# Three chunks loaded in float32 by another queue, one burst of column tiles, and an instruction order from a list scheduler that runs when the program is built, in a fused retention and feed-forward kernel

## The chip, the cores and the metric

The kernel runs on one core of one Trainium2 chip. Times are device microseconds (us) of one execution; with one core, the slowest core is that core. Before the change the median of four timed runs was 247.65 us (247.22 to 248.03). The span of a profile, from the first to the last instruction, is 1 to 3 us shorter than the time of its run.

The engines are called PE (TensorE, matmuls), ACT (ScalarE), DVE (VectorE), POOL (GpSimd) and SP (SyncE, here only an issuer of DMAs). "Granted clock" is the share of full TensorE clock that the profile records. Time without a record counts as full, so read it with care: in the traces the first record lies at 27 to 45 us, and until about then matmuls run at about half pace (four 128-column ones last 0.61 us and later 0.39).

## The reference, cut to what matters

```python
def _attn_ref(q, k, v):                       # 4 x 8 heads x 768 x 64, f32
    gamma = 1.0 - 2.0 ** (-5.0 - np.arange(H))
    for t in range(S):                        # retention, one step at a time
        state = gamma * state + k_t (outer) v_t
        y[:, :, t] = scale * q_t @ state

def _moe_ref(x, w_in, w_out, alpha):          # 3072 tokens, 512 -> 2048 -> 512
    h = x @ w_in
    s = np.sin(alpha * h)
    g = h + s * s / (alpha + 1e-09)
    return g @ w_out
```

(Shortened here.) Both kernels cut the sequence into 24 chunks of 128 tokens. Inside a chunk the recurrence becomes matmuls: q and k are scaled by powers of gamma, both are transposed ("T"), the scores k·q are masked ("A"), the mix is scores·v plus q·state ("Y"), and the state takes k·v on ("S"). The chunks then go through the feed-forward in groups of up to four (512 tokens): per group 16 *input slots* of four matmuls each (into `ph`), a sine and a square on ACT, a sum on DVE (into `gT`), and per chunk 16 *output* matmuls (into `po`).

## The kernel before

The parts that the change and the argument touch; cuts are marked with `# ...`.

```python
groups = [2, 4, 4, 4, 4, 4, 2]
# ...
def load_chunk(j):                            # q, k, v of one chunk: POOL issues, cast to bf16 on the way
    # ...
    for name, src in (("q", q), ("k", k), ("v", v)):
        t = big.tile([128, H, D], BF16, name=f"{name}r", tag=f"{name}r", bufs=NJ)
        nc.gpsimd.dma_start(out=t, in_=src[b, :, c * C:(c + 1) * C, :].rearrange("h s d -> s h d"))
# ...
def stage_Y(j):                               # mix: state part on the full array, then score part in column tiles
    # ...
    if c > 0:
        for p in range(NP):
            nc.tensor.matmul(py[:, p, :], s_bd[c % 2][:, p, :], st["qkT", j][:, p, :], ...)
    for p in range(NP):
        for e in range(2):
            nc.tensor.matmul(py[64 * e:64 * e + 64, p, :], raw["v", j][:, 2 * p + e, :], st["aT", j][:, e, p, :], ...)
    # ...
# ...
loads = [w_in 0..3], chunks 2 3, [w_out 0 1], chunks 4 5, [w_out 2 3], chunks 6.. # (shortened)
# ...
for g in range(NG + 1):                       # the instruction order: input slots and output matmuls alternate,
    # ...
    for i in range(FF):                       # and the stages T, A, Y, S of the next group are spread between them
        if g < NG:
            ph = ff_in(g, i)
            s = ff_act(g, i, ph)
        lo, hi = na * i // FF, na * (i + 1) // FF
        for j, sidx in att[lo:hi]:
            if sidx == 0:
                if loads:
                    loads.pop(0)()
                if j + 1 < NJ:
                    stage_scale(j + 1, nc.vector if j + 1 < 6 else nc.gpsimd)
            stages[sidx](j)
        if g < NG:
            ff_add(g, i, ph, s)
        if g > 0:
            # ...
            ff_out(g - 1, i * n, n)
```

Two things to keep in mind: the order in which each engine gets its instructions is fixed when the program is built, and each engine runs its own in order. An instruction that has to wait holds up everything behind it on that engine.

## Time and profile before

| | before |
|---|---|
| median time | 247.65 us (four runs) |
| span of the profile, mean granted clock | 246.4 us, 0.986 |
| PE busy | 217.6 us (88%) |
| first matmul / first input slot | 11.01 / 21.69 us |
| ninth chunk's transposes on PE | 66.05 us |
| last 36 output matmuls | 234.38 to about 242.3 us |

The page of the profile cuts the span into 40 slices. A digit is the busy share of a slice in tenths; PEclk is the granted clock in tenths of full speed.

```profile
PE   0146748799999999999999999999999999999993
PEclk9999986999999999999999999999999999999999
DMA  9999999999998879849957965901101110012112
```

PE is at 9 tenths from about the ninth slice on (a slice is 6.2 us). Before that it waits, and in that time the DMA engines are full. The sixth and seventh slice show a stretch at a lower clock (34.75 to 41.6 us in the clock records).

The chain of work that ended last, followed back from the end, gives shares of the span:

```profile
PE 72%; DMA 12%; ACT 5%; POOL 5%; issue 2%; DVE 2%; POOLq 0%
```

So PE is the limit for most of the span, and DMA with POOL for the start. What one chunk costs PE is read from the timeline of PE. Columns: start, duration, engine, line, operation, output and inputs, count, and in brackets the idle time before it with what ended it.

```profile
106.36 0.39 PE L134 MATMUL pt<-ident,qs 128*128 128x128 bf16 x4
...
106.81 1.03 PE L218 MATMUL po<-w_out,gT 128*128 128x512 bf16 x4
107.67 1.03 PE L195 MATMUL ph<-xT,w_in 128*128 128x512 bf16 x4
108.63 0.40 PE L145 MATMUL pa<-qkT 64*128 64x128 bf16 x8
...
113.10 0.39 PE L176 MATMUL ps<-vr,ks 128*128 128x128 bf16 x4
...
115.05 0.39 PE L134 MATMUL pt<-ident,qs 128*128 128x128 bf16 x4
```

From one transposition to the next is 115.05 - 106.36 = 8.69 us. Four long matmuls take 0.86 us from start to start (107.67 - 106.81), and the eight such blocks of a chunk 6.9 us; about 1.77 us is left for T, A, Y and S. The scores at 108.63 start 0.96 us after the block ahead of them and not 0.86: 0.10 us is lost where PE goes from the full array to 64-row tiles.

The timeline of POOL shows the loads of the start. A DMA that has to wait names the DMA that it waited for:

```profile
8.83 3.04 POOL L74 DMA_DIRECT2D w_in<-in_moe_w_in_dram  x4
11.83 0.92 POOL L66 DMA_DIRECT2D qr<-in_q_dram  x1
...
17.02 0.88 POOL L66 DMA_DIRECT2D vr<-in_v_dram  x1 [0.78 <-DMA w_in<-in_moe_w_in_dram]
19.53 0.75 POOL L77 DMA_DIRECT2D w_out<-in_moe_w_out_dram  x1 [1.62 <-DMA w_in<-in_moe_w_in_dram]
```

Counted through, the DMA at 17.02 us is POOL's sixteenth and waits for its eighth; the next waits for its ninth. So in these traces POOL has no more than eight of its DMAs under way: an issue can be held until the eighth one before it has landed, and POOL, being in order, does nothing else while it is held.

### The profile page before, as it was taken

What the parts mean: (1) busy time and instruction counts of PE and PEld (TensorE: products, weight loads), DVE (VectorE), ACT (ScalarE), POOL (GpSimd) and SP (SyncE); (2) the same over time, 40 slices, a digit from 0 to 9 for tenths busy, and PEclk for the clock granted to TensorE, in tenths of its full rate; (3) what the DMA queues carried; (4) which work ended last, traced back from release to release, by engine and by line L of the source; (5) the groups of instructions that cost most, each with busy time, mean ns of one, the idle gap of its engine ahead of it and who ended that gap; (6) DMA issues with size and microseconds to landing.
All of it is one profiled execution on the core that took longest, in us unless ns stands there. A gap on an engine that the chain in (4) does not pass through costs nothing.

```text
span 246.4 us, 4059 instructions
## 1 busy us (share of the span) xinstructions
PE 217.6 (88%) x1568; PEld 115.8 (47%) x1568; DVE 132.8 (54%) x208; ACT 172.1 (70%) x294; POOL 108.5 (44%) x127
## 2 busy tenths in 40 slices
PE   0146748799999999999999999999999999999993
PEld 0134436544554555445555544555454454466541
DVE  0444646675666654674475466447645556353431
ACT  2325458889888887778778776877877786877710
POOL 8974754899977733763574376303000000000000
PEclk9999986999999999999999999999999999999999
DMA  9999999999998879849957965901101110012112
GB/s 53 117 205 177 193 164 194 118 95 78 88 133 55 92 85 67 87 66 72 99 67 85 64 80 73 80 26 45 43 0 47 43 43 22 23 43 85 45 43 85
DMA packets 84642, 20.18 MB, mean 82 GB/s; under 512 B 77456, under 2 KB 81552, under 8 KB 84624
## 3 DMA queue, kind: packets, MB, share of 16 engines
q0 software_dynamic: 79104, 13.64, 70.6%
q1 hardware_dynamic: 5520, 6.30, 7.3%
q8 instruction: 12, 0.20, 0.3%
q14 instruction: 6, 0.05, 0.1%
HBM read 27.27 MB, written 6.29 MB: 136 GB/s over the span
## 4 chain that ended last, share of the span: by engine, by line
PE 72%; DMA 12%; ACT 5%; POOL 5%; issue 2%; DVE 2%; POOLq 0%
PE po L218 33%; PE ph L195 29%; DMA w_out<-in_moe_w_out_dram 5%; DMA w_in<-in_moe_w_in_dram 4%; DMA vr<-in_v_dram 3%; PE pt L134 3%; PE py L163 3%; ACT s L202 3%; PE pa L145 2%; ACT s L203 2%; PE py L159 1%; POOL qr L66 1%; PE ps L176 1%; POOL kr L66 1%; DVE gT L207 1%
## 5 line engine op out<-in xcount | busy, mean ns | idle before, releaser
L207 DVE TENSOR_TENSOR gT<-ph,s 128x512 bf16<-128x512 f32 (+1 forms) x112 | 68.7, 613 | 83.5 <-ACT s L203 83.5
L195 PE MATMUL ph<-xT,w_in 128*128 128x512 bf16 (+1 forms) x448 | 104.6, 358 | 2.1 <-DVE gT L207 1.8
L202 ACT ACTIVATE s<-ph,alpha_sb 128x512 f32<-128x512 f32 (+1 forms) x112 | 70.0, 625 | 42.9 <-PE ph L195 30.8
L218 PE MATMUL po<-w_out,gT 128*128 128x512 bf16 x384 | 98.9, 380 | 0.0
L203 ACT ACTIVATE s<-s,rsq_alpha 128x512 f32<-128x512 f32 (+1 forms) x112 | 74.0, 661 | 3.6
L195 PEld LDWEIGHTS <-w_in 128*128 128x128 bf16 x448 | 44.3, 101 | 47.4 <-issue 4.4
L218 PEld LDWEIGHTS <-gT 128*128 128x128 bf16 x384 | 33.2, 98 | 29.1
L126 POOL TENSOR_TENSOR qs<-qr,qg 128x512 bf16<-128x512 bf16 x18 | 18.9, 1050 | 50.5 <-issue 46.1
L148 DVE TENSOR_TENSOR aT<-pa,mask 128x1024 bf16<-128x1024 f32 x24 | 29.3, 1221 | 4.6 <-PE pa L145 4.6
L66 POOL DMA_DIRECT2D qr<-in_q_dram x24 | 22.5, 938 | 1.3 <-POOLq L280 0.8
L66 POOL DMA_DIRECT2D vr<-in_v_dram x24 | 21.7, 905 | 0.8 <-DMA w_in<-in_moe_w_in_dram 0.8
L66 POOL DMA_DIRECT2D kr<-in_k_dram x24 | 21.6, 899 | 0.0
L134 PE MATMUL pt<-ident,qs 128*128 128x128 bf16 x96 | 10.2, 234 | 11.8 <-DVE qs L126 11.7
L166 ACT CAST xT<-py 128x512 bf16<-128x512 f32 x24 | 13.7, 570 | 9.8 <-PE py L163 9.8
L222 DVE COPY o_sb<-po 128x512 f32<-128x512 f32 x24 | 16.4, 681 | 5.0 <-PE po L218 5.0
L127 POOL TENSOR_TENSOR ks<-kr,kg 128x512 bf16<-128x512 bf16 x18 | 18.8, 1043 | 0.0
L136 DVE COPY qkT<-pt 128x1024 bf16<-128x1024 bf16 x24 | 16.4, 682 | 2.5 <-PE pt L134 2.4
L145 PE MATMUL pa<-qkT 64*128 64x128 bf16 x192 | 10.4, 233 | 7.5 <-DVE qkT L136 7.5
L134 PEld LDWEIGHTS <-qs 128*128 128x128 bf16 x96 | 7.8, 105 | 16.9 <-DVE qs L126 12.2
L182 ACT CAST s_bd<-ps 64x256 bf16<-64x256 f32 x40 | 14.3, 359 | 0.3
L145 PEld LDWEIGHTS <-qkT 64*128 64x128 bf16 x192 | 5.9, 100 | 17.0 <-DVE qkT L136 11.9
L163 PE MATMUL py<-aT,vr 128*64 128x128 bf16 x192 | 10.8, 239 | 3.0 <-DVE aT L148 2.4
(32 smaller groups left out, 77.1 us busy)
## 6 DMA issues: line engine op xcount, KB each, us to landing
out_dram<-o_sb SPq DMA_DIRECT2D x24, 256.0 KB, 2.0
qr<-in_q_dram POOLq DMA_DIRECT2D x24, 128.0 KB, 3.6
kr<-in_k_dram POOLq DMA_DIRECT2D x24, 128.0 KB, 4.4
vr<-in_v_dram POOLq DMA_DIRECT2D x24, 128.0 KB, 4.4
w_in<-in_moe_w_in_dram POOLq DMA_DIRECT2D x4, 512.0 KB, 8.0
w_out<-in_moe_w_out_dram POOLq DMA_DIRECT2D x4, 512.0 KB, 10.4
alpha_sb<-in_moe_alpha_dram SPq DMA_DIRECT2D x1, 8.0 KB, 3.0
```

The source lines that it names most:

```text
L66: nc.gpsimd.dma_start(out=t, in_=src[b, :, c * C:(c + 1) * C, :].rearrange("h s d -> s h d"))
L126: eng.tensor_mul(qs, raw["q", j], qg[:, c, :, None].to_broadcast([128, H, D]))
L127: eng.tensor_mul(ks, raw["k", j], kg[:, c, :, None].to_broadcast([128, H, D]))
L134: nc.tensor.transpose(pt[:, i * NP + p, :], t[:, 2 * p:2 * p + 2, :].rearrange("p h d -> p (h d)"), ident)
L145: nc.tensor.matmul(pa[:, e, p, :], qkT[r, NP + p, :], qkT[r, p, :], start=(p == 0), stop=True, skip_group_check=True)
L148: nc.vector.tensor_mul(aT.rearrange("p e n t -> p (e n) t"), pa.rearrange("p e n t -> p (e n) t"), mask_bc)
L163: nc.tensor.matmul(py[64 * e:64 * e + 64, p, :], raw["v", j][:, 2 * p + e, :], st["aT", j][:, e, p, :], start=(c == 0 and p == 0), stop=Tr ...
L195: nc.tensor.matmul(ph, w_in[:, i, f * 128:(f + 1) * 128], xT[g][:, i, :], start=(i == 0), stop=(i == KS - 1))
L202: nc.scalar.activation(out=s, in_=ph, func=ACTF.Sin, scale=alpha_sb[:, f:f + 1])
L203: nc.scalar.activation(out=s, in_=s, func=ACTF.Square, scale=rsq_alpha[:, f:f + 1])
L207: nc.vector.tensor_add(gT[g][:, f, :], ph, s)
L218: nc.tensor.matmul(po[g], gT[g][:, f, ts * C:(ts + 1) * C], w_out[:, f, :], start=(f == 0), stop=(f == FF - 1))
```

## The change

The intent, by its parts: (1) the first three chunks come in float32 through SP's queue, so that POOL need not issue them (POOL then scales their k and casts their v, DVE scales their q, and ACT copies their transposes, which DVE did before); (2) groups 3,4,4,4,4,4,1 instead of 2,4,4,4,4,4,2; (3) scores, mix and state of a chunk follow one another on PE, with mix and state in column tiles; (4) the order of all instructions comes from a list scheduler in the kernel's own code, which keeps a clock per engine from a simple cost model as it emits; (5) the square of a slot goes to DVE where the scheduler's clock has ACT far behind, and the last copy is split between DVE and ACT. With this, `ph` and `po` share four PSUM buffers, where each had two of its own.

The diff, cut to its core (cuts marked with `...`, some lines joined; most of the stage functions, the PSUM pools and the constants are left out):

```diff
+class Clock:
+    ...
+    def run(self, eng, us, *deps):
+        start = max([self.t[eng]] + [d + 0.1 for d in deps])
+        self.t[eng] = start + us
+        return start + us + (0.15 if eng == "PE" else 0.05)
+def mm_us(n, k=1): return k * (n / 2400 + 0.0025)
+def act_us(n):     return 0.19 + n / 1200
+def dve_us(n):     return 0.13 + n / 960
...
-    groups = [2, 4, 4, 4, 4, 4, 2]
+    groups = [3, 4, 4, 4, 4, 4, 1]
...
+    NEAR = 3
+    def lands(key, us):                      # model of a landing: no wait of the issuer in it
+        dma["t"] += us
+        landed[key] = dma["t"] + 2.3
...
+            if j < NEAR:
+                t = big.tile([128, H, D], F32, name=f"{name}f", tag=f"{name}f", bufs=NEAR)
+                nc.sync.dma_start(out=t, in_=chunk_of(src, j))
+            else:
+                t = big.tile([128, H, D], BF16, name=f"{name}r", tag=f"{name}r", bufs=NJ - NEAR)
+                nc.gpsimd.dma_start(out=t, in_=chunk_of(src, j))
...
+        for t, r, w in ((ks, "k", kg), (qs, "q", qg)):
+            eng, name, us = (nc.vector, "DVE", 0.65) if near and r == "q" else (nc.gpsimd, "POOL", 1.05)
+            eng.tensor_mul(t, raw[r, j], w[:, c, :, None].to_broadcast([128, H, D]))
+            ...
+        if near:
+            ...
+            nc.gpsimd.tensor_copy(vb, raw["v", j])
...
             for p in range(NP):
-                nc.tensor.matmul(py[:, p, :], s_bd[c % 2][:, p, :], st["qkT", j][:, p, :],
+                for e in range(2):
+                    r = slice(64 * e, 64 * e + 64)
+                    nc.tensor.matmul(py[r, p, :], s_bd[c % 2][:, p, r], qkT[:, p, :],
...
+    AHEAD = 4
+    for j in range(NEAR):
+        scale_chunk(j)
+    ...
+    nc.gpsimd.tensor_scalar_add(rec_alpha, alpha_sb, 1e-9)
+    nc.vector.reciprocal(rec_alpha, rec_alpha)
+    nc.scalar.activation(out=rsq_alpha, in_=rec_alpha, func=ACTF.Sqrt)
+    for fn in loads[:8]:                     # w_in, the fourth chunk, w_out 0 1, the fifth chunk
+        fn()
...
+    while go < NG:
+        ...                                  # candidates (time ready, priority, kind): T 0, AM 1, A or M 2, I (input) 3, O (output) 4
+        elif "I" in ready and "O" in ready:
+            ...                              # by progress and by ACT's backlog
+        elif ready:
+            kind = min(ready.values(), key=lambda x: x[1])[2]
+        else:
+            kind = min(cand)[2]
+        ...                                  # emit it
+        while scaled < NJ and scaled <= jT + 1:
+            while loads and ("c", min(scaled + AHEAD, NJ - 1)) not in landed:
+                loads.pop(0)()
+            scale_chunk(scaled)
+            scaled += 1
```

## The prediction

> **What bounds the kernel now.** The table by slices shows TensorE at 9 tenths from about 80 us on; the chain of waits is all PE from there to 242 us, with a 4 us tail (copy, output DMA). In that stretch four 128x512 matmuls take 0.86 us start to start, and a chunk (T, A, Y, S plus its feed-forward) repeats every 8.69 us, 6.9 of it feed-forward and about 1.77 attention. Summed over the kernel that is an estimated 206 us of TensorE work. So some 36 us are lost in the first 80 us: the first matmul starts at 11.0 us, and until about 52 us the PE waits for chunks (the timeline shows w_in landing in quarters every 2.5 us to 22.0 us, a chunk costing 2.55 us of DMA, q of the seventh chunk landing at 43.9 us).
>
> **What the change does.**
> 1. Attention on the PE. The timeline shows 0.10 us extra on each side of row-tiled scores and column-tiled mix; the Trainium skill ("TensorEngine Tiling (Array Packing)", Key Properties) says that a change of tiling mode drains the array, and the trace agrees. State and mix in one column-tiled burst after the scores should make 1.77 us about 1.6: 3.5 us less PE work. This lies on the critical path.
> 2. Groups 3,4,...,1: more feed-forward early. Split last copy: 0.3 us.
> 3. First three chunks through SyncE: POOL's six issues (0.9 us each) go. The data still cost about 0.85 us of DMA per tensor (an estimate; no run shows it yet).
> 4. What is given back. POOL now scales k and casts v of these chunks and needs alpha, the tenth SyncE DMA, before it issues w_in. I estimate that at 12.5 to 13 us, against 8.83 us before. Then it issues everything up to the eighth chunk before it scales the fourth. The waits before show that a POOL DMA waits for the landing of the eighth one before it; so the issue of that chunk's v waits for q of the sixth, some 29.5 us after w_in's issue. Scaling of the fourth chunk starts near 43.5 us, and then each chunk costs POOL 3 issues and 2 multiplies, 4.7 us (as before between 44 and 70 us). Before, VectorE scaled chunks up to the sixth, and the ninth was scaled at 55.6 us; now it is ready near 69 us.
> 5. The instruction order of the PE is fixed from a model without these waits: the fourth chunk's transposes stand after 8 of the first group's 16 input slots, so the PE should idle from about 23 to 45 us with work at hand, then follow POOL's pace until the ninth chunk's transposes, near 69 us.
>
> After that point the order still holds an estimated 172.4 us of PE work (664 long matmuls, 143 us). 69 + 172.4 + 3.7 = 245, plus an estimated 3 us in which dense input slots run at ScalarE's pace (1.41 us against 0.86 on PE). What faster attention and a fuller start save, POOL takes back.
>
> **Predicted: 248 us**, 8 in 10 within 240 to 257. Faster by over 2%: 0.2; within 2%: 0.54; slower: 0.26.
>
> **What would show it.** w_in issue on POOL near 13 us; a PE gap of about 20 us before transposes that wait for a POOL multiply; POOL's 4.7 us rhythm to about 90 us; the chain of waits made of DMA and POOL up to about 69 us, then PE; attention near 1.6 us per chunk.
>
> **What would make it wrong.** SyncE loads off 0.85 us each; column tiles not running in pairs; ScalarE limiting more groups, or none, after 69 us; a cold PE clock after the gap.

## The result, and the profile after

Ratios in this document are the mean time of one kernel's fast runs over the mean of the other's of the same rounds, so they are not quite the ratio of the medians that are quoted.

| | before | after |
|---|---|---|
| median time | 247.65 us | 266.88 us (265.88 to 268.39) |
| ratio | | 1.0782 (95%: 1.0725 to 1.0839), slower |
| span, mean granted clock | 246.4 us, 0.986 | 264.2 us, 0.961 |
| PE busy | 217.6 us | 218.6 us |
| first input slot | 21.69 us | 27.97 us |
| ninth chunk's transposes | 66.05 us | 74.90 us |
| time at the end in which the last group runs | | 233.93 to 259.99 us |

The changed kernel is 7.8% slower, and its time lies outside the predicted range of 240 to 257 us.

The page of the profile after, same rows:

```profile
PE   1036940699699889999999999999999899987993
PEclk9999995599999999999999999999999999997799
DMA  8959999999999999997901100101011011111022
```

A slice is now 6.6 us. There is a hole in PE in the sixth to eighth slice (about 36 to 49 us), a stretch at about half clock in the seventh and eighth, and near the end a second dip, with PE at 8 and 7 and then the clock at 7 and 7. The clock records put the slow stretches at 39.5 to 53.2 us and 240.9 to 247.7 us. The chain of work that ended last has less PE and more ACT than before:

```profile
PE 61%; DMA 12%; ACT 10%; issue 6%; POOL 3%; DVE 3%; SPq 3%; DVEq 0%
```

The timeline of POOL shows how the start went:

```profile
5.36 1.04 POOL L171 TENSOR_TENSOR ks<-kf,kg 128x512 bf16<-128x512 f32 x1 [2.33 <-DMA kf<-in_k_dram]
...
8.90 1.04 POOL L171 TENSOR_TENSOR ks<-kf,kg 128x512 bf16<-128x512 f32 x1 [1.82 <-DMA kf<-in_k_dram]
...
12.52 1.04 POOL L171 TENSOR_TENSOR ks<-kf,kg 128x512 bf16<-128x512 f32 x1 [1.83 <-DMA kf<-in_k_dram]
...
15.10 3.25 POOL L117 DMA_DIRECT2D w_in<-in_moe_w_in_dram  x4
...
44.63 0.88 POOL L108 DMA_DIRECT2D kr<-in_k_dram  x1 [1.65 <-DMA w_out<-in_moe_w_out_dram]
45.59 0.88 POOL L108 DMA_DIRECT2D vr<-in_v_dram  x1
46.48 1.06 POOL L171 TENSOR_TENSOR ks<-kr,kg 128x512 bf16<-128x512 bf16 x1
47.48 1.04 POOL L171 TENSOR_TENSOR qs<-qr,qg 128x512 bf16<-128x512 bf16 x1
```

The float32 chunks come every 3.6 us, 1.2 us a tensor (12.52 - 5.36 over six tensors), so w_in is issued only at 15.10 us. Then POOL issues loads up to the eighth chunk (its v at 45.59 us) and scales the fourth only after that, at 46.48 us, although that chunk had been issued at 18.30 us. PE pays for it. This is the timeline of PE:

```profile
16.53 0.61 PE L201 MATMUL pa<-qkT 64*128 64x128 bf16 x8 [9.46 <-ACT qkT L188]
...
27.97 7.83 PE L261 MATMUL ph<-xT,w_in 128*128 128x384 bf16 x32 [0.46 <-ACT xT L237]
48.59 0.61 PE L184 MATMUL pt<-ident,qs 128*128 128x128 bf16 x4 [12.78 <-POOL qs L171]
...
233.93 0.61 PE L261 MATMUL ph<-xT,w_in 128*128 128x128 bf16 x8
...
239.55 0.38 PE L261 MATMUL ph<-xT,w_in 128*128 128x128 bf16 x4 [0.30 <-DVE gT L281]
240.24 0.38 PE L261 MATMUL ph<-xT,w_in 128*128 128x128 bf16 x4 [0.31 <-DVE gT L281]
240.93 3.34 PE L261 MATMUL ph<-xT,w_in 128*128 128x128 bf16 x20 [0.30 <-DVE gT L281]
244.37 15.62 PE L305 MATMUL po<-w_out,gT 128*128 128x512 bf16 x64
```

Line by line: the first scores wait 9.46 us for a copy on ACT; the first group gets 8 of its 16 input slots (32 matmuls), then PE stands still for 12.78 us before the fourth chunk's transposes, for a multiply on POOL. At the end the last group, of one chunk, runs its sixteen 128-wide input slots almost without output matmuls between them, at 0.69 us a slot (240.24 - 239.55), and the 64 output matmuls left over come after them in one burst of 15.62 us, 0.244 us each, where long matmuls take 0.215 us elsewhere: the burst begins in the second slow stretch.

The view of waits has the cause of the first of these:

```profile
ACT rsq_alpha L334 <- DVE rec_alpha L333: 11.6, 1, 11.6
```

ACT's square root of alpha stands in its stream ahead of the copies of the first chunks' transposes. It needs POOL's small sum on alpha, which stands behind the third chunk's cast. So ACT does nothing for 11.6 us and PE's first scores wait for it.

### The profile page after: what moved, and what is told of

Read it like the earlier page. It is cut to its first block, busy times and chain, and to the rows that moved or that the text cites. A ratio compares the mean times of both kernels' runs of the same rounds, so it can differ in the third digit from the quotient of the medians.

```text
span 264.2 us, 4365 instructions
## 1 busy us (share of the span) xinstructions
PE 218.6 (83%) x1728; PEld 113.5 (43%) x1728; DVE 127.6 (48%) x196; ACT 170.4 (64%) x297; POOL 112.1 (42%) x131
## 4 chain that ended last, share of the span: by engine, by line
PE 61%; DMA 12%; ACT 10%; issue 6%; POOL 3%; DVE 3%; SPq 3%; DVEq 0%
PE po L305 30%; PE ph L261 22%; ACT s L264 7%; DMA w_out<-in_moe_w_out_dram 5%; DMA w_in<-in_moe_w_in_dram 5%; PE pt L184 3%; SPq L105 3%; PE pa L201 2%; DMA vf<-in_v_dram 2%; PE py L220 2%; ACT s L270 2%; PE py L224 2%; DVE gT L281 1%; ACT xT L237 1%; POOL w_in L117 1%
## 5 line engine op out<-in xcount | busy, mean ns | idle before, releaser
L261 PE MATMUL ph<-xT,w_in 128*128 128x512 bf16 (+2 forms) x448 | 102.5, 364 | 6.0 <-DVE gT L281 4.7
L281 DVE TENSOR_TENSOR gT<-ph,s 128x512 bf16<-128x512 f32 (+2 forms) x112 | 68.8, 614 | 77.1 <-ACT s L270 76.7
L264 ACT ACTIVATE s<-ph,alpha_sb 128x512 f32<-128x512 f32 (+2 forms) x112 | 69.2, 618 | 43.2 <-PE ph L261 37.2
L305 PE MATMUL po<-w_out,gT 128*128 128x512 bf16 x384 | 95.2, 385 | 0.1
L270 ACT ACTIVATE s<-s,rsq_alpha 128x512 f32<-128x512 f32 (+2 forms) x111 | 73.4, 661 | 3.6
L171 POOL TENSOR_TENSOR ks<-kr,kg 128x512 bf16<-128x512 bf16 x21 | 22.3, 1064 | 30.7 <-PE ps L233 27.8
L171 POOL TENSOR_TENSOR qs<-qr,qg 128x512 bf16<-128x512 bf16 x21 | 22.2, 1056 | 5.4 <-issue 5.4
L237 ACT CAST xT<-py 128x512 bf16<-128x512 f32 x24 | 13.7, 573 | 12.9 <-PE py L224 12.9
L108 POOL DMA_DIRECT2D vr<-in_v_dram x21 | 18.8, 894 | 4.9 <-DMA w_in<-in_moe_w_in_dram 3.0
L108 POOL DMA_DIRECT2D kr<-in_k_dram x21 | 18.6, 884 | 4.4 <-DMA w_out<-in_moe_w_out_dram 2.8
L220 PE MATMUL py<-qkT,s_bd 128*64 128x128 bf16 x160 | 9.3, 234 | 2.2 <-DVE qkT L191 1.1
```

The source lines that it names most:

```text
L108: nc.gpsimd.dma_start(out=t, in_=chunk_of(src, j))
L171: eng.tensor_mul(t, raw[r, j], w[:, c, :, None].to_broadcast([128, H, D]))
L237: nc.scalar.copy(xT[g][:, :, o:o + C], py)
L261: nc.tensor.matmul(ph, w_in[:, i, f * 128:(f + 1) * 128], xT[g][:, i, :], start=(i == 0), stop=(i == KS - 1))
L264: nc.scalar.activation(out=s, in_=ph, func=ACTF.Sin, scale=alpha_sb[:, f:f + 1])
L270: nc.scalar.activation(out=s, in_=s, func=ACTF.Square, scale=rsq_alpha[:, f:f + 1])
```

## The experiments

The theory after reading the trace: the loss has two separate causes, both in the instruction order. *Look-ahead*: AHEAD = 4 makes POOL issue everything up to the eighth chunk before it scales the fourth, and its DMAs are held by the eight-under-way limit, so PE gets its chunks late. *Tail*: where neither kind of slot is ready in the model, `min(cand)` breaks a tie of the time by priority, which puts input slots before output slots; in the last group, whose slots are only 128 wide, ACT limits input slots, and nothing is left to fill PE with.

Rivals: the column-tile burst is slower than its parts were; w_in's late issue (15.1 us instead of 8.83) sets the time, not the look-ahead; ACT's early stand over alpha sets it; float32 loads through SP cost more than they save; a wrong cost model spoils the order everywhere.

All kernels gave correct results. "Time" is the median of fast runs, "ratio" is to the kernel before on the same chip in the same rounds.

| run | time, us | ratio to before (95%) |
|---|---|---|
| e1_tail | 259.59 | 1.0462 (1.0439 to 1.0485) |
| e2_ahead | 254.89 | 1.0303 (1.0266 to 1.0339) |
| e3_both | 248.29 | 1.0023 (0.9996 to 1.0050) |
| e4_oldmix | 251.37 | 1.0142 (1.0115 to 1.0170) |
| e5_win | 256.93 | 1.0377 (1.0341 to 1.0414) |
| e6_alpha | 249.21 | 1.0061 (1.0038 to 1.0084) |
| e7_alpha_win | 259.28 | 1.0452 (1.0420 to 1.0484) |
| e8_model | 249.72 | 1.0083 (1.0053 to 1.0112) |
| e9_alpha_dve | 248.19 | 1.0027 (1.0008 to 1.0046) |
| e10_swdge | 244.00 | 0.9846 (0.9831 to 0.9860) |
| e11_best | 244.41 | 0.9868 (0.9834 to 0.9902) |
| e12_tail_again | 259.16 | one run, no interval |

The differences between experiments below are differences of these ratios, times 247.9 us.

### e1_tail: break the tie for the output slots in the last group

```diff
-            kind = min(cand)[2]
+            kind = min(cand, key=lambda x: (x[0], -x[1] if gi == NG - 1 else x[1]))[2]
```

PE's order differs from that of after only in the last group: its last burst of output matmuls is 24 long instead of 64.

> The changed kernel, except that in the last group the scheduler's tie goes to output work instead of input work; the order differs only in the last 64 narrow input matmuls and the last 48 output ones. Theory (the sixteen 128-wide input slots run alone at ScalarE's 0.69 us a slot, 7.4 us more than TensorE needs, and the clock falls to one half for 6.8 us, 3.4 us lost): about 9 to 10 us less than the changed kernel, so near 257 us, and no half clock before the final output matmuls. Rival (narrow slots are dear wherever they stand, or the clock falls for another reason): less than 3 us less.

Measured: three fast runs, 258.71 to 259.87 us, 7.9 us less than after by the ratios. The fourth run, the one that was profiled, took 456.81 us: its PE was busy for 419 us, and four long matmuls took 1.88 us instead of 0.86 in every stage, so about half the pace throughout. The 1.0 given as its granted clock says nothing against that: its trace holds no clock record at all (its page has no row PEclk). It is left out. The mechanism had to be read from e12_tail_again below, the same file run again.

### e2_ahead: look ahead one chunk instead of four

```diff
-    AHEAD = 4
+    AHEAD = 1
```

The orders on PE, ACT, DVE and SP are the same as in after, instruction by instruction; only POOL's changes. This makes it a clean test of the look-ahead.

> The changed kernel, except that POOL issues the loads only one chunk ahead of the chunk that it scales instead of four; the order of TensorE, ScalarE, VectorE and SyncE is the same line by line. Theory (POOL reaches the fourth chunk's multiply only at 46.5 us because it issues four more chunks first, each DMA waiting for the landing of the eighth before it): the fourth chunk's transposes start near 33 us instead of 48.6, the ninth chunk's near 63 us instead of 74.9, and the time falls by 9 to 12 us to about 256. Rival (the fourth chunk is late because the late w_in and the DMA queue itself are slow, whatever POOL does): the fourth chunk's transposes move by less than 4 us and the time by less than 3 us.

Measured: 254.89 us, 11.9 us less than after. The fourth chunk's transposes start at 35.77 us (after: 48.59), the ninth's at 63.45 us (after: 74.90). So the ninth chunk comes 11.45 us earlier, and all of that reaches the end. The tail is the old one, with a dip of the clock near the end again.

### e3_both: the two edits together

> Both edits. If the two losses lie in different stretches of one critical path, they add: about 20 us less than the changed kernel, near 247 us, so level with the kernel before. If one hides the other, less than 14 us.

Measured: 248.29 us, 18.8 us less than after; the two alone add up to 19.8 us. So the two causes are separate and nearly additive, and together they are the net loss against before: the interval of the ratio to before includes 1. In its timeline of POOL the fourth chunk is scaled as soon as its load has landed:

```profile
31.19 1.04 POOL L171 TENSOR_TENSOR ks<-kr,kg 128x512 bf16<-128x512 bf16 x1 [1.66 <-DMA kr<-in_k_dram]
```

The granted clock is 1.0 wherever its trace has a record (from 30.8 us on): both slow stretches of after are gone, with the waits ahead of them. The Trainium skill ("TensorE: Matmul & The Clock Gate", Part 1, What's actually happening) states two clock states, half and full, and a fall to half after about 3.4 us of idling. The trace of after agrees: 12.78 us of idle time and a stretch of 13.7 us at a low clock that begins 3.7 us into it; the records here also show the dip of 6.8 us in the tail, where PE was never idle for more than 0.95 us at a time but had only 0.22 us of matmuls in each slot of 0.69 us.

### e5_win: w_in issued right after the first chunk's scaling

```diff
-    for j in range(NEAR):
+    scale_chunk(0)
+    for fn in loads[:4]:
+        fn()
+    for j in range(1, NEAR):
         scale_chunk(j)
...
-    for fn in loads[:8]:
+    for fn in loads[4:8]:
```

This is e3_both with one block moved. It tests the rival that w_in's late issue sets the time.

> As e3_both, and POOL issues the four w_in loads after the first chunk's multiply and cast instead of after all three chunks and alpha, so near 7 us instead of 15.1. Theory (w_in waits behind POOL work while the DMA engines run dry for about 3.5 us; every later landing moves with it): the fourth chunk's transposes 2 to 4 us earlier than in e3_both and the time 2 to 4 us less, near 244. Rival (TensorE sets the pace by then): less than 1 us.

Measured: 256.93 us, 8.8 us more than e3_both, although w_in was issued at 7.05 us instead of 15.19. The third chunk's k was multiplied only at 19.57 us and alpha's sum came at 25.13 us; the first scores started at 26.87 us (e3_both: 16.62). What w_in gained, the float32 chunks behind it lost. So an early w_in does not help by itself. The run also held ACT for alpha for longer, and e6 and e7 were made to take that apart.

### e4_oldmix: the old mix and state matmuls in the new burst

```diff
-                for e in range(2):
-                    r = slice(64 * e, 64 * e + 64)
-                    nc.tensor.matmul(py[r, p, :], s_bd[c % 2][:, p, r], qkT[:, p, :],
+                nc.tensor.matmul(py[:, p, :], s_bd[c % 2][:, p, :], qkT[:, p, :],
...
-                for e in range(2):
-                    nc.tensor.matmul(ps[64 * e:64 * e + 64, p, :], st["ks", j][:, 2 * p + e, :], vb[:, 2 * p + e, :],
+                nc.tensor.matmul(ps[:, p, :], st["ks", j][:, 2 * p:2 * p + 2, :]..., vb[:, 2 * p:2 * p + 2, :]..., 
```

> As e3_both, but with the matmuls of the kernel before in the mix and the state (four 128-column ones each instead of eight column tiles), in the same places of the same order. Theory (column tiles run in pairs and spare the changes of tiling mode inside the burst): attention burst longer by 0.2 to 0.4 us a chunk, so 4 to 9 us more than e3_both. Rival (no gain from the tiles, TensorE waits for others): within 1.5 us of e3_both.

Measured: 251.37 us, 2.95 us more than e3_both. The timeline of PE of e3_both, one chunk from its scores to the next long block:

```profile
120.43 0.40 PE L201 MATMUL pa<-qkT 64*128 64x128 bf16 x8
120.75 0.41 PE L220 MATMUL py<-qkT,s_bd 128*64 128x128 bf16 x8
121.00 0.39 PE L224 MATMUL py<-aT,vr 128*64 128x128 bf16 x8
121.22 0.29 PE L233 MATMUL ps<-vr,ks 128*64 128x64 bf16 x8
121.45 1.04 PE L305 MATMUL po<-w_out,gT 128*128 128x512 bf16 x4
```

and the same of e4_oldmix:

```profile
123.06 0.40 PE L201 MATMUL pa<-qkT 64*128 64x128 bf16 x8
...
124.30 1.03 PE L303 MATMUL po<-w_out,gT 128*128 128x512 bf16 x4
```

The burst takes 1.02 us in column tiles and 1.24 us in the old form, 0.22 us a chunk. Over 24 chunks that would be 5.3 us; 2.95 us of it reached the end, since some of the chunks, the early ones above all, have idle time of PE to hide it in (the ninth chunk came 2.0 us later than in e3_both; the rest of the run took 2.2 us longer). Not all of this is the tiles': the profile of e4_oldmix has a low clock from 61.37 to 64.78 us, which that of e3_both has not, and it made the matmuls there an estimated 1.4 us longer. Between the runs of both with a granted clock of 0.997 and more (250.76 and 250.81 us against 247.92 to 248.40) the difference is 2.6 us. So the part of the change that was meant to be faster is faster, and the rival that it costs time falls. The Trainium skill ("TensorEngine Tiling (Array Packing)", Key Properties) states that a change of tiling mode drains the array; the traces agree with 0.10 us at each such change.

### e6_alpha: alpha loaded ahead of the chunks

```diff
-    for j in range(NEAR):
-        load_chunk(j)
     alpha_sb = consts.tile([128, FF], F32, name="alpha_sb")
     nc.sync.dma_start(out=alpha_sb, in_=moe_alpha.rearrange("(fo fi) -> fi fo", fi=128))
+    for j in range(NEAR):
+        load_chunk(j)
```

> As e3_both, but SyncE loads alpha before the three chunks instead of after them. ScalarE's square root of alpha then no longer stands before the first transposed chunk's copy, and POOL's w_in issue no longer waits for alpha. Theory (the order of every engine is fixed, so one late small DMA holds the first three chunks' attention for 9.5 us, and the first group's input work starts at 28.1 us although the first quarter of w_in is there near 21): the scores of the first chunk at about 8 us instead of 16.6, the first input matmul near 21 to 22, the time 3 to 6 us less than e3_both. Rival (POOL's chain sets the pace until 60 us anyhow): less than 1.5 us less.

Measured: 249.21 us, ratio 1.0061 against 1.0023 for e3_both: no gain. The edit missed its target: POOL still made alpha's sum after the third chunk's cast (at 15.79 us), so ACT was held as before and the first scores came at 17.54 us. It tells nothing about ACT's stand; e9 does.

### e7_alpha_win: alpha first and w_in early

The edit of e5_win on top of e6_alpha.

> As e6_alpha, and w_in issued after the first chunk's multiply and cast. This mends what e5_win broke if what broke it was alpha's DMA landing at 24.9 us behind w_in: then it is at least as fast as e6_alpha and 12 us or more faster than e5_win. Rival (w_in in flight beside the chunks slows the chunks themselves and that is what cost 8 us in e5_win): 3 us or more slower than e6_alpha.

Measured: 259.28 us, 9.7 us more than e6_alpha. Its timeline of POOL:

```profile
9.05 3.22 POOL L117 DMA_DIRECT2D w_in<-in_moe_w_in_dram  x4
...
21.22 1.04 POOL L171 TENSOR_TENSOR ks<-kf,kg 128x512 bf16<-128x512 f32 x1 [6.86 <-DMA kf<-in_k_dram]
26.60 0.61 POOL L175 CAST vb<-vf 128x512 bf16<-128x512 f32 x1 [4.34 <-DMA vf<-in_v_dram]
```

With w_in under way, the third chunk's k is 8.7 us later than in after (12.52 us), although it is issued by another engine. The Trainium skill ("DMA: Bandwidth & Descriptors", Issuing engines are not separate DMA queues) states that DMAs of all issuers run on the same 16 DMA engines and interleave; this agrees. The test is not clean: alpha's sum still stood on POOL behind these waits (27.30 us), so ACT was held until then, and how much of the 9.7 us each of the two takes is not separated. That the chunks arrive late is shown; that it alone costs 9.7 us is not.

### e8_model: measured costs in the scheduler

On top of e6_alpha:

```diff
 def act_us(n):
-    return 0.19 + n / 1200
+    return 0.28 + n / 1200
 def dve_us(n):
-    return 0.13 + n / 960
+    return 0.155 + n / 960
...
+            if issue:                        # POOL: each DMA behind the landing of the eighth before it
+                start = clk.t["POOL"]
+                if len(issued) >= 8:
+                    start = max(start, issued[-8])
+                clk.t["POOL"] = start + issue
+            dma["t"] = max(dma["t"], start + 1.9) + us / parts
+            landed[key] = dma["t"] + 1.3
```

> As e6_alpha, but the scheduler's durations and landing times are set from the traces: ScalarE 0.28 us plus n/1200, VectorE 0.155 us plus n/960, POOL's DMA issues of 0.9 and 0.79 us, each behind the landing of the eighth before. Theory (the order is only as good as the model it was made with: it places the narrow and wide input slots at a pace that ScalarE cannot hold, and POOL's work earlier than it comes): 3 to 6 us less than e6_alpha, and fewer waits of input matmuls for VectorE's adds. Rival (the order hardly matters once POOL and the tail are mended): within 1.5 us of e6_alpha.

Measured: 249.72 us, 0.5 us more than e6_alpha. The ninth chunk came later (66.40 against 64.28 us), and the time from there to the end was shorter (183.16 against 184.58 us). The two orders are not at the same point there: by the ninth chunk's transposes e8_model had put 20 more long matmuls behind it, about 4.3 us of work. So the start was better by an estimated 2.2 us and the rest worse by 2.9: from there to the last matmul PE was idle for 6.9 us, against 4.1 in e6_alpha. A better model moved the loss from one place to another; it was not the lever here.

### e9_alpha_dve: alpha's sum and root ahead of the chunks, off POOL

On top of e6_alpha:

```diff
-    for j in range(NEAR):
-        scale_chunk(j)
     rec_alpha = ...
-    nc.gpsimd.tensor_scalar_add(rec_alpha, alpha_sb, 1e-9)
+    nc.vector.tensor_scalar_add(rec_alpha, alpha_sb, 1e-9)
     nc.vector.reciprocal(rec_alpha, rec_alpha)
     nc.scalar.activation(out=rsq_alpha, in_=rec_alpha, func=ACTF.Sqrt)
+    for j in range(NEAR):
+        scale_chunk(j)
```

> As e3_both, alpha loaded first, and its sum and reciprocal on VectorE before the first chunk's multiplies, so that neither POOL's multiplies nor alpha's landing stand before ScalarE's square root. In e6_alpha this wait stayed, because POOL did the sum after the third chunk's cast. Theory: the first scores now start near 8 to 9 us instead of 17.5, the first input matmul near 21 to 22 instead of 29, yet the time falls by only 1 to 3 us against e3_both, because from the fourth chunk on POOL and the landings set the pace (its transposes can't start before 33 to 34 us). Rival (the nine lost microseconds at the start are on the critical path): 6 us or more less than e3_both.

Measured: 248.19 us, within 0.1 us of e3_both by the ratios. The timeline of PE:

```profile
9.69 0.61 PE L201 MATMUL pa<-qkT 64*128 64x128 bf16 x8 [1.10 <-ACT qkT L188]
...
33.50 0.40 PE L184 MATMUL pt<-ident,qs 128*128 128x128 bf16 x4 [2.25 <-POOL qs L171]
```

The first scores start 6.9 us earlier than in e3_both, the first input slot at 23.42 instead of 28.06 us, and it is worth nothing: PE now waits for the fourth chunk's multiply on POOL, and the ninth chunk's transposes start at 63.59 us, about as in e3_both (63.28). ACT's stand over alpha was real and stood out in the view of waits, but it was not on the path. The path at the start is landings and POOL.

### e10_swdge: the first three chunks through POOL again, in bf16

On top of e9_alpha_dve:

```diff
-            if j < NEAR:
-                t = big.tile([128, H, D], F32, name=f"{name}f", tag=f"{name}f", bufs=NEAR)
-                nc.sync.dma_start(out=t, in_=chunk_of(src, j))
-            else:
-                t = ...
-                nc.gpsimd.dma_start(out=t, in_=chunk_of(src, j))
+            t = big.tile([128, H, D], BF16, name=f"{name}r", tag=f"{name}r", bufs=NJ)
+            nc.gpsimd.dma_start(out=t, in_=chunk_of(src, j))
...
+            if near:
+                eng = nc.vector              # q and k of these chunks; v needs no cast
```

> As e9_alpha_dve, with the change's loading of the first three chunks undone: POOL loads them as bf16, VectorE scales q and k of them, no cast of v. Theory (through SyncE each tensor took 1.15 to 1.2 us in f32, against 0.85 through POOL, and POOL then multiplied before it issued w_in): w_in issued near 12 us instead of 15, everything that POOL and the DMA queue pace 3 us earlier, so 2 to 4 us less than e9_alpha_dve, though the first transposes start near 11 us instead of 6. Rival (the SyncE loads are a gain, since POOL is spared nine issues of 0.9 us): slower than e9_alpha_dve by 1 us or more.

Measured: 244.00 us, 4.5 us less than e9_alpha_dve and 1.5% less than before, with the whole interval below 1. It is the fastest kernel, though within 2% of before. Its timeline of POOL:

```profile
11.53 3.04 POOL L113 DMA_DIRECT2D w_in<-in_moe_w_in_dram  x4
...
27.77 1.04 POOL L169 TENSOR_TENSOR ks<-kr,kg 128x512 bf16<-128x512 bf16 x1 [1.99 <-DMA kr<-in_k_dram]
```

PE's order is the same as in e9_alpha_dve and its first scores are later (14.07 against 9.69 us), but w_in is issued at 11.53 instead of 15.56 us, the fourth chunk is scaled 3.6 us earlier, and the ninth chunk's transposes start at 59.48 us, 4.1 us earlier than in e9_alpha_dve. Some 1.7 us of the 4.1 are a low clock that e9_alpha_dve has from 41.74 to 45.16 us and e10_swdge has not (an estimate from the matmuls there); e3_both has none either, and e10_swdge is 4.4 us faster than that too. So the loads through SP, with the scaling and casts that go with them, were themselves a loss. The Trainium skill ("DMA: Bandwidth & Descriptors", Issuing engine by pattern) says that a DMA issued by SP or ACT is "generally faster" than one of POOL. Per tensor the measurement is the other way round: about 1.2 us in float32 through SP, an estimated 0.85 us in bf16 through POOL (from a chunk's 2.55 us in the trace before). But a float32 tensor writes 256 KB and a bf16 one 128 KB, so per byte written SP was the faster. The two differ in the type written as well as in the issuer, and no run takes these apart.

### e11_best: everything that looked useful, and VectorE for the first eight chunks

On top of e10_swdge: the model of e8, and DVE scales every chunk below the ninth once the model says it has landed.

```diff
-            eng, name, us = (nc.vector, "DVE", 0.65) if near and r == "q" else (nc.gpsimd, "POOL", 1.05)
+            eng, name, us = (nc.vector, "DVE", 0.68) if j < 8 else (nc.gpsimd, "POOL", 1.05)
...
+        if NEAR <= scaled < NDVE and scaled <= jT + 1:
+            soon = min(x[0] for x in cand) if cand else 1e9
+            if not cand or landed["c", scaled] - 0.3 <= max(now, soon):
+                scale_chunk(scaled)
+                scaled += 1
+                continue
```

> What the runs so far point to together: the order of the tail, alpha first and on VectorE, the first three chunks through POOL, chunks up to the eighth scaled by VectorE when they have landed, POOL free to issue, and the scheduler's model set from the traces. Theory (what is left of the loss is POOL's 4.7 us a chunk and the late w_in): the ninth chunk's transposes near 55 us instead of 63, the time 238 to 243 us, faster than both kernels. Rival (the DMA engines or ScalarE set the pace whatever POOL does): 246 us or more.

Measured: 244.41 us, not different from e10_swdge (their intervals overlap). The ninth chunk's transposes started at 59.33 us, not near 55. POOL no longer scales these chunks, and PE still gets them at the same time. This alone is no clean test, since the order changed too, but in the view of waits of e10_swdge PE waits only 0.2 us in all for POOL's multiplies; so they do not limit e10 any more. What does there (landings, ACT, or both) was not tested.

### e12_tail_again: e1_tail once more, for a profile

> The same kernel as e1_tail, once more, only because the profiled execution of e1_tail was an odd one (455 us, every stage stretched). Theory: no 3 us stretch in which narrow input matmuls wait alone, no half clock between 230 us and the end, and the last 24 output matmuls at 0.215 us each; but the first 75 us as in the changed kernel, the ninth chunk's transposes near 75 us. Rival (the gain of e1_tail came from elsewhere): the half clock is still there in the tail.

Measured: one run (so its state is unknown), 259.16 us, in agreement with the fast runs of e1_tail. Its ninth chunk comes at 74.50 us, as in after, so only the tail differs. The timeline of PE there:

```profile
233.53 0.61 PE L261 MATMUL ph<-xT,w_in 128*128 128x128 bf16 x8
233.98 0.81 PE L305 MATMUL po<-w_out,gT 128*128 128x512 bf16 x3
...
246.64 0.81 PE L305 MATMUL po<-w_out,gT 128*128 128x512 bf16 x3
247.28 0.39 PE L261 MATMUL ph<-xT,w_in 128*128 128x128 bf16 x4
247.51 5.34 PE L305 MATMUL po<-w_out,gT 128*128 128x512 bf16 x24
```

From the first narrow slot to the end of the last burst is 233.53 to 252.85 us, 19.3 us; in after it is 233.93 to 259.99 us, 26.1 us, for the same slots. (A few matmul records are missing from this trace; groups of x3 are of four.) The clock stays full to the end, where after had 6.8 us at half clock. The 6.7 us gained are the output matmuls that now fill the narrow slots' waits, and that clock. No run takes the two apart, but an estimate does: 64 long matmuls in one burst at full clock would last about 14.0 us (63 starts at 0.216 us and 0.38 for the last), so the low clock made some 1.6 us of the 15.62, and the filled waits the rest. The expectation of e1_tail had put the clock at 3.4 us; but half of the slow stretch lies in narrow slots, which came every 0.69 us at either clock.

### What all profiles say together

In the profiled runs, the time from the ninth chunk's transposes to the end (time of the run minus start of these transposes; a run of another order has done other work by then) is:

| profiled run | ninth chunk, us | rest, us |
|---|---|---|
| after, e2_ahead (old tail) | 74.90, 63.45 | 191.0, 190.4 |
| e12_tail_again | 74.50 | 184.7 |
| e3_both, e6_alpha, e9_alpha_dve | 63.28, 64.28, 63.59 | 184.6, 184.6, 184.6 |
| e5_win, e7_alpha_win | 71.94, 74.64 | 184.6, 184.6 |
| e10_swdge, e11_best | 59.48, 59.33 | 184.3, 184.5 |
| e4_oldmix (old mix) | 65.31 | 186.8 |
| e8_model (other order) | 66.40 | 183.2 |
| before (other order, old mix) | 66.05 | 182.1 |

The rest stays at 184.3 to 184.7 us for every kernel with the mended tail and the same order, while the ninth chunk moves over 15 us. So a microsecond that the start loses before the ninth chunk is lost in full, and the old tail costs about 6 us more, whatever the start was.

## Why the prediction was wrong

The prediction said 248 us, the kernel took 266.88. Its sum was 69 + 172.4 + 3.7 + 3, and it is best compared with the profile's span of 264.2 us; the time of a run lies 1 to 3 us above the span, a difference that the prediction did not make and that is the smallest of the errors. The two terms that failed are the 69 (the ninth chunk; 74.90 measured) and the 3 (waits after it; about 13), and with them the balance "What faster attention and a fuller start save, POOL takes back": POOL's look-ahead alone took 11.9 us, and the tail, which is in no term, about 8.

1. **The mechanism at the start was right.** The predicted chain was: POOL reaches w_in late; then it issues everything up to the eighth chunk before it scales the fourth; the eighth chunk's v waits for q of the sixth, some 29.5 us after w_in. The trace has w_in at 15.10 us and the eighth chunk's v at 45.59 us, 30.5 us later, with the fourth chunk's scaling right behind it at 46.48 us. PE waited for a POOL multiply before the fourth chunk's transposes, as predicted, for 12.78 us; the predicted gap of "about 20 us" was too long because the first input slots started at 27.97 us and not at the predicted time. POOL's rhythm was 4.69 us a chunk. e2_ahead, which changes POOL's order alone, shows that this was worth 11.9 us. The prediction saw that what the change saves "POOL takes back", but it took the balance for about nothing.

2. **The step "the ninth is ready near 69 us" was mis-sized: 74.90 us.** Its first term, w_in's issue at "12.5 to 13 us", was 15.10 us: the prediction costed a float32 tensor through SP at 0.85 us, which was an estimate from POOL's bf16 loads, and it took about 1.2 us. e10_swdge shows that the loads are a loss in themselves, 4.5 us with the scaling and casts that go with them. The second term is PE: POOL had scaled the ninth chunk at 72.0 us, PE reached its transposes 2.9 us later. In sum 5.9 us of the error.

3. **The step "plus an estimated 3 us in which dense input slots run at ScalarE's pace" failed: it was about 13.** From 74.90 us to the end of the span are 189.3 us, where the prediction had 172.4 + 3.7 + 3 = 179.1. The largest piece is the tail, which the prediction never costed: a last group of one chunk has 128-wide slots, in which PE has 0.22 us of work and ACT 0.69. The timeline of ACT after,

```profile
239.77 0.35 ACT L264 ACTIVATE s<-ph,alpha_sb 128x128 f32<-128x128 f32 x1
240.15 0.40 ACT L270 ACTIVATE s<-s,rsq_alpha 128x128 f32<-128x128 f32 x1
240.46 0.35 ACT L264 ACTIVATE s<-ph,alpha_sb 128x128 f32<-128x128 f32 x1
```

   shows the pace: from one sine to the next 0.69 us. A sine of 512 columns takes 0.68 us on average and one of 128 takes 0.35, so a quarter of the width costs more than half of the time. The scheduler's tie rule then put nothing of the output work between. The same order also let the clock fall for 6.8 us. e1_tail gains 7.9 us with the tie broken the other way, and the table of rests gives 6.3 us (191.0 - 184.7). The remaining 3.4 to 4 us after the ninth chunk, which e3_both has too, are waits of the kind predicted, but more of them. The prediction's 172.4 us of PE work holds: 664 long matmuls at 0.216 us, 64 narrow ones at 0.056 and 16 chunks at 1.56 make an estimated 172. In e3_both PE takes 178.3 us from the ninth chunk's transposes to the end of its last matmul, so some 6 us are waits, where 3 were predicted. The timeline has them as idle times of mostly 0.3 to 1.0 us before input matmuls that wait for DVE's sums, and before one chunk's transposes that wait for a copy by ACT. No run took these waits away.

4. **The cheaper attention was right.** The predicted 1.6 us a chunk was measured as 1.02 us for the burst, 0.10 ahead of it and 0.44 for the transposes, 1.56 in sum. e4_oldmix shows it on the clock: 2.95 us for the column tiles alone, against a predicted 3.5 us for the whole of attention.

5. **Not foreseen, and harmless:** ACT's stand of 11.6 us over alpha. e9_alpha_dve removes it and gains nothing.

6. **What was named as a risk:** "a cold PE clock after the gap" came, for 13.7 us, of which PE worked at a low clock from 48.59 to 53.2 us; "SyncE loads off 0.85 us each" came too. Both were in the text as doubts, and neither was in the range.

Why was the change no gain even with both faults mended (e3_both, 1.0023)? Not because of the start: by the table of rests e3_both is 2.8 us ahead of before at the ninth chunk's transposes, with slightly more of the feed-forward done (an estimated 19.0 against 18.2 us of matmuls). The gain is lost after that: the rest takes 184.6 us against 182.1, though the cheaper attention should save it an estimated 3.4 us (16 chunks at 0.21). Cut into windows, 157 us from the ninth chunk on in before and then in e3_both (start and end, length, then busy time of PE, PEld, DVE, ACT and POOL, clock, DMA share and GB/s):

```profile
66.05:223.05 157.00, 156.53 (x1103) 79.06 (x1102) 91.35 (x130) 123.52 (x202) 57.16 (x61) 1.00 0.56 63
63.28:220.28 157.00, 153.34 (x1212) 76.82 (x1211) 92.03 (x128) 125.11 (x203) 66.89 (x72) 1.00 0.63 63
```

PE is idle for 0.5 us in before and for 3.7 us in e3_both. The same reckoning as under 3 gives before about 176 us of matmuls in 176.3 us, so next to no waits, where e3_both has some 6 us. So the scheduler's order brings waits that the fixed alternation of before did not have; what in it does so was not tested, nor were the groups or the shared PSUM buffers by themselves. The loads through SP cost about 4.5 us more. With those undone, e10_swdge has a gain at last, 244.00 us against 247.7.

## What to carry to other kernels

When an order comes from a scheduler, look at what breaks its ties and at what its model leaves out: here one tie rule cost about 8 us and one look-ahead constant 12, and both were one-line edits. Compare its order with the one that it replaces also where both look busy: here it left an estimated 6 us of waits that the old order did not have. An engine that both issues loads and prepares data should issue only as far ahead as its DMAs can go without being held, because behind a held issue everything stands. And cost the last group by itself: a narrow group is limited by the fixed costs of the engines that were hidden in the wide ones, so it needs other work between its slots.

## What the Trainium skill lacked or had wrong

- "DMA: Bandwidth & Descriptors", Issuing engine by pattern, calls DMAs of SP and ACT "generally faster". Per tensor it was not so here, though per byte written it was: the first three chunks took about 1.2 us a tensor (float32, through SP) against an estimated 0.85 us (bf16, through POOL), and the kernel with POOL's loads was 4.5 us faster (e10_swdge against e9_alpha_dve). Type and issuer changed together (256 KB written a tensor against 128 KB), so the page is not shown wrong.
- The same page, Issuing engines are not separate DMA queues, calls the issuing time "usually small relative to the DMA itself". SP's issues of these loads grew from 0.43 us for the first to 1.02 to 1.15 us from the fourth on, about the 1.2 us at which the tensors arrived. Whether the issue sets that pace or is held by it, the runs don't tell.
- No page that was read tells that POOL's DMA issue is held in such a program until the eighth one before it has landed; here an issue was held up to 3.24 us before and 2.98 us after, and with a look-ahead of four chunks it cost 11.9 us (e2_ahead). Whether the chip or the program asks for it, the runs don't tell.
- "TensorE: Matmul & The Clock Gate", Part 1, tells of a fall to half clock after an idle window of about 3.4 us, and of a kernel whose clock swings with micro-idles between groups of matmuls (A second HAM failure mode: psum-queue depth-cycling), without their length. Here it fell with no idle time of 3.4 us behind it: in the tail of after for 6.8 us, where PE was never idle for more than 0.95 us at a time, but worked some 0.22 us out of each 0.69; in before at 34.75 us, 1.6 us into an idle time of 2.88 us; and in e9_alpha_dve at 41.74 us, after one of 2.53 us.
